# The shift of a modulation in PSUM columns of its own, without idle products, and a new hand-written job order in an attention and MLP kernel

## The chip, the cores and the metric

The kernel runs on one core of one Trainium2 chip. The metric is the time of one execution on the device, in microseconds. Five engines work beside each other, each through its own instructions in order: TensorE (PE, matrix products into PSUM), VectorE (DVE), ScalarE (ACT), GpSimd (POOL) and SyncE (SP), whose queue issues nearly all DMA transfers. PSUM has 8 banks of 512 fp32 columns.

## The reference

One transformer block with a modulation computed from a vector c. S = 2048 rows, D = 576 features, H = 32 heads of 18, Dff = 4608:

```
mod = silu(c) @ w_mod            # six vectors of 576: sa, ca, ga, sb, cb, gb
h = layernorm(x) * (1 + ca) + sa
q, k, v = split(h @ wqkv)        # per head, 18 wide
pq, pk = q @ w_phi, k @ w_phi    # per head, 18 x 18
phi_q = [softmax(pq), softmax(-pq)] ; phi_k likewise
kv = phi_k^T v ; z = sum over rows of phi_k
o = (phi_q kv) / (phi_q z + 1e-6) ; x = x + ga * (o @ wo)
h = layernorm(x) * (1 + cb) + sb
x = x + gb * (relu(h @ w1) @ w2)
```

## The kernel before, in words

The rows are 16 tiles of 128. The first part (up to about 90 us) is attention, the second (line 720 on) an MLP of eight blocks of two tiles, with two levels of a seven-product scheme. The change lies in the first part.

**Folded weights.** w_phi is folded into the Q and K weights on PE: `FK` (line 444, `fold_all`) makes the folded K weights in PSUM in 25 products, five for each of five chunks of features; `frd` and `fra` (line 455) copy chunk n to SBUF on DVE or ACT, `frr` (line 662) copies the rest of all chunks. `FQ n` (line 262) does the same for chunk n of Q, copied by `FQrd` or `FQra` (line 562).

**The norm without a normalized x.** x is loaded twice: in rows (`Lx..`, for the statistics `bn` on DVE, lines 243 and 244) and turned, features on partitions (`Lt0` to `Lt4`, for products). The turned x is multiplied by 1 + ca only, in place (`xd`, `xa`, `xp` on DVE, ACT or POOL, line 548, for two tiles at a time). Mean and standard deviation enter through four extra rows of the last of the five chunks of the contraction: on the x side they come from the statistics (`sa` on ACT, `sp` on POOL, `T` a transposition on PE, `Tc` a copy on ACT), on the weight side from products of the small matrix `m98` with the weights (`KR`, `VR`, `QR`, lines 273 and 369), whose rows are then put together by `KRh`, `KRd` and their like (lines 514 and 518). `m98` holds -(1 + ca) three times and the shift sa once (columns 96 to 99).

**The modulation.** `sx` (ACT) and `sd` (DVE, line 538) make silu(c). `sc` and `sh` (line 250, `mods`) are 25 products of one column each, for the scale ca and the shift sa, both into columns 0 to 4 of PSUM bank 7; ahead of each five of them stands an idle product of 512 columns (`spin`, line 236) into bank 6, which nothing reads. `ca` (line 543) reads the scale out of bank 7, adds 1, and writes -(1 + ca) to `m98`. `shc` (line 659) copies the shift to `m98`. `Z11` and `Z1` are idle products as well. The second modulation (`m2`, line 677) is made later.

**Tiles.** For each tile t: `K t` are ten products of 288 columns (line 279), `eK` two Exps on ACT (line 285), `sK` sums on DVE (line 291), `rK` reciprocals on ACT (line 307), `pA` and `pM` products on POOL, `V t` ten products, `vE` a product out of PSUM on DVE (line 312), `kv` nine products that accumulate over all tiles in banks 6 and 7, `Q t`, `eQ` like K. K of tile 0 and 1 is split: `Ka` (the first four chunks, eight products) and `Kb` (the last chunk, two products, which need the extra rows).

**What sets the order.** `ORDER` (line 45) is a list written out by hand; line 709 runs the jobs in that order, and each engine gets its instructions in it. `X:n` gives the job two PSUM banks, pair n. Semaphores are put in by the framework: an instruction waits for the writers of what it reads, and for the readers of what it overwrites. A load on SP also waits until the load eight places ahead of it on its ring has landed.

Of the kernel before, what the change touches and what calls it, by code (L numbers as in the profile page):

```python
# [18 lines left out]
NC = 5  # L19
R = 116  # L20
F = NC * R
FP = NC * F + P - R
X0 = 96
# [19 lines left out]


ORDER = """
Lbdw Z11 LwkT FK Z1 fra1 Lx0 Lcc sx bn0 sd frd2 Lwsc frd0 bn1 sa0 frr sc ca Lwsh frd4 Lx2 Lid bn3 sh fra3 sp0 T0:1 shc
Lt0 KR:2 KRh0 Lwv Lx4 xd0 bn2 KRh1 mk KRd0 KRd1 Tc0 sa2 Ka0:0 VR:1 bn4 VRh0 Kb0 VRd0 sp2 VRh1 Lt1 xd2 Ka1:2 Kb1 VRd1
T2:1 eKa0 sK0 LwqT FQ3:3 Tc2 K2:0 FQra3 bn5 Lwsb eKa1 sK1 K3:3 rK0 eK2 sa4 FQ4:2 FQrd4 pM0 V0:1 sK2 Lwcb rK1 pA1 pA0
Lt2 pM1 V1:0 m2:2 eK3 FQ0:3 Lx6 vE0 V2:1 Lwga vE1 rK2 Lx10 m2c FQrd0 pA2 FQ1:3 xa4 sp4 Lt4 bn7 vE2 T4:2 Tc4 K4:0 FQra1
eK4 FQ2:2 xp6 bn6 sa6 FQrd2 sK3 Lt3 bn11 K5:1 pM2 kv0 kv1 QR:2 eK5 V3:0 kv2 QRh sp6 QRe QRd T6:2 rK3 sK4 pA3 vE3 rp  # L50
Tc6 pM3 K7:1 rK4 K6:2 pM4 pA4 eK7 eK6 Lwgb ga:0 gac V4:1 bn9 kv3 sK5 rK5 bn8 pA5 w2b0 sa8 V5:2 vE4 bn12 sp8 T8:0 xa8
pM5 vE5 Tc8 Q0:1 eQ0 gb:2 xp14 kv4 kv5 sK6 bn10 Q1:0 gbc sa10 sK7 gaw gar wl1 rK6 K8:1 qs0 wl3 bn15 eQ1 eK8 K9:2 eK9
sp10 xp10 Lwo Q2:0 pA6 sK8 pM6 eQ2 V6:1 rK8 bn13 vE6 sK9 bn14 qp0 rK7 Q3:2 pA8 T10:0 Tc10 pA7 eQ3 qs1 pM7 kv6 K10:1
eK10 rK9 K11:0 sK10 pM8 V8:2 eK11 sa14 sa12 V7:1 vE8 pM9 rK10 V9:0 vE7 xa12 sp12 pA9 kv7 T12:2 sK11 rK11 kv8 V10:1 vE9
kv9 wl0 pA10 vE10 Tc12 pM10 K12:0 sp14 T14:2 Tc14 gbw eK12 kv10 K13:1 eK13 wo2 K14:2 eK14 qt0 qs2 sK12 sK13 Q4:0 eQ4
rK13 K15:1 w2a1 qp1 V11:2 V12:0 gbr qs3 wo1 pA11 qp2 pM11 vE11 kv11 w2a2 rK12 w2a0 pA12 eK15 vE12 sK15 pM12 qt1 V13:2
kv12 pM13 Lmask sK14 Q5:1 wl4 rK15 eQ5 sq5 Q6:0 pA13 pA15 vE13 sq4 kv13 qt2 V15:2 rK14 vE15 pM15 pA14 V14:1 vE14 eQ6
Q11:2 pM14 qp3 sq6 kv14 kv15 qt3 eQ11 sq11 Q7:1 kz nu1:2 Q8:0 nu0:3 nO1 td2 eQ7 eQ8 sq7 nO0 td0 sq8 ot1:2 td1 Q9:1 oc1
Q10:0 ot0:2 wo0 wo4 eQ9 qi5 wo3 sq9 oc0 eQ10 W1:3 xr1 qi4 W0:1 lb1 Q12:2 xr0 lb0 Q13:0 lr1 eQ12 sq10 qi6 lr0 ap1 eQ13
Q14:1 ht1:2 Q15:3 ap0 wl2 ht0:0 ha eQ14 eQ15 hd w2b1 sq13 sq15 sq14 sq12  # L60
"""

SEVEN = """
# [18 lines left out]
def tile_block(ctx, tc, a, out):  # L82
# [7 lines left out]
    def small(shape, dtype, name):  # L90
        return mem.tile(shape, dtype, name=name, tag=name)

    def carve(reg, start, shape):
        n = 1
        for d in shape:
            n *= d
        names = "abcd"[:len(shape)]
        v = reg[:, start:start + n]
        return v.rearrange(f"p ({' '.join(names)}) -> p {' '.join(names)}", **dict(zip(names, shape)))
# [21 lines left out]
    wsc, wsh, wkT, wqT = (R1[:, i * FP:(i + 1) * FP] for i in range(4))  # L121
# [8 lines left out]
    mk = small([P, 1], FP32, "mk")  # L130
# [4 lines left out]
    sc = carve(early, 1536, (4, P))  # L135
# [7 lines left out]
    m98 = carve(RS, NC * GR, (NC, NX))  # L143
# [28 lines left out]
    PS = psum.tile([P, 8, 512], FP32, name="PS")  # L172
# [6 lines left out]
    act, dve, pool, sp, pe = nc.scalar, nc.vector, nc.gpsimd, nc.sync, nc.tensor  # L179
# [56 lines left out]
    def spin(n, bank, w=512):  # L236
        for _ in range(n):
            pe.matmul(PS[:, bank, 0:w], lhsT=zero[:, 0:P], rhs=zero[:, 0:w], start=True, stop=True)  # L238
# [7 lines left out]
    def wide(w, ck, ci):  # L246
        o = ck * F + ci * R
        return w[:, o:o + P]

    def mods(w, bank, idle=None):  # L250

        o = PS[:, bank, :] if isinstance(bank, int) else bank[:, 0, :]
        for k, wm in enumerate(w):
            for ci in range(NC):
                if idle is not None:
                    spin(1, idle)
                for ck in range(NC):
                    wt = wide(wm, ck, ci) if len(wm.shape) == 2 else wm[:, ck, ci * P:(ci + 1) * P]
                    pe.matmul(o[:, k * NC + ci:k * NC + ci + 1], lhsT=wt[0:R],
                              rhs=siluc[0:R, ck:ck + 1], start=(ck == 0), stop=(ck == NC - 1))  # L260

    def fold_mm(wT, ck, pr):
# [181 lines left out]
    def fold_all(wT):  # L444

        for ck in range(NC):
            for g, (h0, nh) in enumerate(G7):
                nf, c0 = nh * DH, h0 * DH
                o = PS[:, ck, c0:c0 + nf] if g < 4 else PS[:, 5, FW * ck:FW * (ck + 1)]
                pe.matmul(o, lhsT=wide(wT, g, ck)[0:nf], rhs=bdw[0:nf, g, 0:nf], start=True, stop=True,  # L450
                          skip_group_check=True)
# [47 lines left out]
    T1, T2, T4 = (carve(RTh, i * TW, (NK, HD)) for i in range(3))  # L499
# [42 lines left out]

    def scale():
        dve.tensor_scalar(out=ca1[0:R, :], in0=PS[0:R, 7, 0:NC], scalar1=1.0, scalar2=None, op0=ALU.add)
        dve.tensor_scalar(out=m98[0:R, :, X0:X0 + 3], in0=ca1[0:R, :].unsqueeze(2).to_broadcast([R, NC, 3]), scalar1=-1.0,
                          scalar2=None, op0=ALU.mult)

# [94 lines left out]
    def k_minus(t):  # L642
# [10 lines left out]
    JOBS = {  # L653
        "Z": lambda i: spin(i, 6),
        "sx": lambda: act.activation(out=sg[0:R, 0, :], in_=ccol[0:R, :], func=ACT.Exp, scale=-1.0),
        "sd": silu, "ca": scale,
        "sc": lambda: mods([wsc], 7, idle=6),
        "sh": lambda: mods([wsh], 7, idle=6),
        "shc": lambda: dve.tensor_copy(m98[0:R, :, X0 + 3], PS[0:R, 7, 0:NC]),
        "FK": lambda: fold_all(wkT),  # L660
        "frd": lambda c: f_raw(dve, c), "fra": lambda c: f_raw(act, c),
        "frr": lambda: dve.tensor_copy(out=wk[0:R, :, G5:D], in_=last),
# [12 lines left out]
        "Q": lambda t: proj(at["Q", t], t, wq), "eQ": lambda t: exps(t, at["Q", t], EQ[:, SLOT[t], :]),  # L675
        "sq": q_out, "qi": q_in, "qs": q_sm, "qp": q_pool, "qt": q_turn,
        "m2": lambda: mods([wsb, wcb], at["m2", None]), "m2c": lambda: mod2_e(at["m2", None]),
        "wo": lambda c: pool.tensor_tensor(out=wo_sb[:, c, :], in0=wo_sb[:, c, :], in1=ga_row[:], op=ALU.mult),
        "wl": w1_part, "w2a": w2a_part, "w2b": w2b_part,
# [528 lines left out]
```

## Time and profile before

| | us |
|---|---|
| median of 3 runs | 375.18 (374.82 to 376.08) |
| the profiled execution | 374.84 |
| its span, first to last instruction | 373.1 |
| PE busy | 367.7 |
| DVE busy | 282.4 |
| ACT busy | 220.0 |
| first product of the MLP (line 732) starts at | 90.68 |

The page gives the busy time of each engine and 40 slices of the span; the chain of work that ended last tells, at each moment, whose work the end hung on; the timeline gives single instructions, with the idle time before them and what ended it in brackets. PE's matrix products are pipelined: two that follow each other start 0.12 us apart at 288 columns, though each is shown as 0.29 us long. The last slice of PE is not full because the output is added and written after the last product.

### The profile page before, as it was taken

To read this page: it belongs to the slowest core of one execution; us is meant where nothing else is said; L and a number is where in the kernel's file an instruction comes from. 1 tells how busy PE (TensorE), PEld (TensorE's weight loads), DVE (VectorE), ACT (ScalarE), POOL (GpSimd) and SP (SyncE) were. 2 spreads that over 40 slices of the span, in tenths; PEclk is the share of its full clock that TensorE was granted. 3 is DMA by queue.
4 is the path that set the end of the run, shared out by engine and by line. 5 is a ranking of instruction groups with operands and counts; after the bars stand their busy time and mean duration, and the time that the engine had idled before them with its cause. 6 is when DMAs were issued, how large, how long until landed. Compare 5 with 4: busy or idle time off the path is not lost.

```text
span 373.1 us, 14298 instructions
## 1 busy us (share of the span) xinstructions
PE 367.7 (99%) x6245; PEld 313.6 (84%) x6245; DVE 282.4 (76%) x508; ACT 220.0 (59%) x495; POOL 138.9 (37%) x203
## 2 busy tenths in 40 slices
PE   8999999999999999999999999999999999999996
PEld 4787888888888788889988987898799889979975
DVE  2999998679979779987795688578668747745752
ACT  2598998588633435608752774478167608844730
POOL 2167999840302567380054007102600240044023
DMA  8985799887966436463127236512521123101001
GB/s 296 414 362 154 271 411 315 218 238 296 265 187 132 125 81 152 126 133 95 36 46 182 35 35 83 147 37 52 128 52 20 37 50 37 35 0 36 4 2 33
DMA packets 58591, 49.96 MB, mean 134 GB/s; under 512 B 46880, under 2 KB 50848, under 8 KB 57760
## 3 DMA queue, kind: packets, MB, share of 16 engines
q1 hardware_dynamic: 58384, 48.88, 48.1%
q8 instruction: 49, 0.80, 0.9%
q10 hardware_dynamic: 144, 0.16, 0.1%
q14 instruction: 14, 0.11, 0.1%
HBM read 31.98 MB, written 5.90 MB: 102 GB/s over the span
## 4 chain that ended last, share of the span: by engine, by line
PE 96%; DVE 1%; ACT 1%; issue 0%; POOL 0%; DVEq 0%; POOLq 0%
PE PS L878 33%; PE PS L798 23%; PE PS L282 15%; PE PS L732 10%; PE PS L946 4%; PE PS L781 3%; PE PS L401 2%; PE PS L331 2%; PE PS L238 1%; PE PS L276 1%; PE PS L953 1%; PE PS L418 1%; PE PS L918 1%; ACT R L558 1%; DVE RH L459 0%; DVE st L243 0%
## 5 line engine op out<-in xcount | busy, mean ns | idle before, releaser
L878 PEld LDWEIGHTS <-RH 128*128 128x128 f16 x846 | 81.7, 98 | 21.2 <-issue 0.4
L866 POOL TENSOR_TENSOR yt<-yt,gb_row 128x288 f32<-128x288 f32 x23 | 27.5, 1194 | 176.1 <-DVE yt L865 176.1
L798 PEld LDWEIGHTS <-R 64*128 64x128 bf16 (+1 forms) x1824 | 76.0, 94 | 0.8 <-issue 0.2
L878 PE MATMUL PS<-R,RH 128*128 128x288 bf16 (+1 forms) x558 | 73.2, 286 | 0.0
L798 PE MATMUL PS<-h,R 64*128 64x128 bf16 x1056 | 69.2, 216 | 0.0
L828 ACT ACTIVATE RH<-PS 128x512 f16<-128x512 f32 x96 | 50.9, 605 | 9.2 <-PE PS L798 9.0
L798 PE MATMUL PS<-RE,R 64*128 64x128 f16 x768 | 48.1, 216 | 0.0
L287 ACT ACTIVATE RT<-PS,rs 128x576 bf16<-128x576 f32 x64 | 42.9, 744 | 3.6 <-PE PS L282 3.4
L878 PE MATMUL PS<-RT,RH 128*128 128x288 f16 x288 | 37.9, 286 | 0.0
L732 PE MATMUL PS<-h,R 64*128 64x256 bf16 (+1 forms) x684 | 36.3, 264 | 0.0
L732 PEld LDWEIGHTS <-R 64*128 64x128 bf16 x684 | 31.6, 94 | 3.9 <-issue 0.2
L975 ACT ACTIVATE h<-h,mod 128x256 bf16<-128x256 bf16 x63 | 32.5, 589 | 1.0 <-DMA h<-xn 1.0
L282 PE MATMUL PS<-RH,R 116*128 116x288 bf16 x240 | 32.7, 286 | 0.1
L798 PE MATMUL PS<-h,early 64*128 64x128 bf16 x384 | 32.0, 216 | 0.0
L282 PE MATMUL PS<-RH,RT 116*128 116x288 bf16 x240 | 31.5, 286 | 0.0
L818 ACT ACTIVATE yt<-PS 128x512 f32<-128x512 f32 x10 | 6.0, 597 | 42.7 <-PE PS L798 41.8
L243 DVE BATCH_NORM_STATS2 st<-x_sb 128x6 f32<-128x288 bf16 x64 | 25.7, 443 | 6.3 <-DMA x_sb<-in_xk_dram 6.2
L865 DVE TENSOR_TENSOR yt<-PS,RS 128x288 f32<-128x288 f32 x23 | 10.5, 456 | 23.4 <-PE PS L878 23.3
L282 PEld LDWEIGHTS <-R 116*128 116x128 bf16 x240 | 22.6, 98 | 6.2 <-ACT R L626 0.4
L282 PEld LDWEIGHTS <-RT 116*128 116x128 bf16 x240 | 22.9, 98 | 5.5
L798 PEld LDWEIGHTS <-w 64*128 64x128 f16 (+1 forms) x480 | 26.4, 94 | 0.0
L867 POOL TENSOR_TENSOR x_sb<-yt,x_sb 128x288 bf16<-128x288 f32 x30 | 24.9, 833 | 3.5 <-DVE yt L863 1.7
(153 smaller groups left out, 737.9 us busy)
## 6 DMA issues: line engine op xcount, KB each, us to landing
R<-in_w_dram SPq DMA_DIRECT2D x4, 1152.0 KB
eqd<-RT SPq DMA_DIRECT2D x12, 288.0 KB, 3.6
RT<-eqd SPq DMA_DIRECT2D x12, 288.0 KB, 3.1
R<-in_w2b_dram SPq DMA_DIRECT2D x2, 1296.0 KB, 6.7
R<-in_w2a_dram SPq DMA_DIRECT2D x3, 864.0 KB
out_dram<-x_sb SPq DMA_DIRECT2D x15, 144.0 KB, 1.8
RT<-in_xT_dram SPq DMA_DIRECT2D x2, 640.0 KB, 6.5
x_sb<-in_xk_dram SPq DMA_DIRECT2D x8, 144.0 KB, 3.6
```

The costliest lines, as they stand in the source:

```text
L243: dve.bn_stats(out=s[:, hf, :], in_=x_sb[:, t % 8 if n else t, hf * HD:(hf + 1) * HD])
L282: pe.matmul(pr[:, k, 0:HD], lhsT=xt(t, ck), rhs=w[0:R, ck, k * HD:(k + 1) * HD], start=(ck == 0), stop=(ck == NC - 1))
L287: act.activation(out=E.rearrange("p (b h s e) -> p b h s e", b=2, s=2, e=DH)[:, :, :, s, :], in_=pr[:, :, 0:HD].rearrange("p b (h e) -> p ...
L732: pe.matmul(PS[:, 2 * u + hf, n * 256 + o:n * 256 + o + w], lhsT=w1_lhs(hf, c, j, h), rhs=hb[b0:b0 + 64, c, o:o + w], start=(n == 0 and c ...
L781: pe.matmul(PS[:, bank_at[n], j * 256:j * 256 + 256], lhsT=w1_lhs(hi, c, j, hi), rhs=hb[64 * hi:64 * hi + 64, c, :], start=(j == 0 and c = ...
L798: pe.matmul(PS[:, bank_at[BK[n] + str(g)], i * P:(i + 1) * P], lhsT=w[r, (4 * c + i) * P:(4 * c + i + 1) * P], rhs=x, start=(n in ("M1", " ...
L828: act.activation(out=o, in_=v[{"k11": "Y", "k12": "Z", "k21": "X", "k22": "W"}[n]], func=ACT.Relu)
L866: pool.tensor_tensor(out=y, in0=y, in1=gb_row[:, c], op=ALU.mult)
L867: eng.tensor_tensor(out=xs(t)[:, c], in0=y, in1=xs(t)[:, c], op=ALU.add)
L878: pe.matmul(PS[:, bank, 0:HD], lhsT=am[:, j, :], rhs=bm[:, j, :], start=first and j == 0, stop=(j % 9 == 8), skip_group_check=True)
L946: pe.matmul(pr[:, k, 0:HD], lhsT=oT[:, t % 2, ci, :], rhs=wo_sb[:, ci, k * HD:(k + 1) * HD], start=(ci == 0), stop=False, skip_group_check ...
L975: act.activation(out=o, in_=o, func=ACT.Identity, scale=mod(1, c), bias=mod(0, c))
```

## The change

It does four things. The idle products of `sh` go. `sh` writes columns 8 to 12 of bank 7 instead of 0 to 4, and `shc` reads them there. The job `ca` is split: `ca` makes 1 + ca, a new job `cm` writes the negated copies to `m98`. And ORDER is a new list, in which among much else the turned x of tiles 0 and 1 (`Lt0`) is loaded ahead of the shift's weights (`Lwsh`), `sx` stands ahead of the fold, the turned x of tiles 4 to 7 (`Lt2`) is loaded ahead of the second modulation's weights, and the first four chunks of K of tile 0 (`Ka0`) come before the m98 products of K (`KR`).

```diff
 ORDER = """
-Lbdw Z11 LwkT FK Z1 fra1 Lx0 Lcc sx bn0 sd frd2 Lwsc frd0 bn1 sa0 frr sc ca Lwsh frd4 Lx2 Lid bn3 sh fra3 sp0 T0:1 shc
-Lt0 KR:2 KRh0 Lwv Lx4 xd0 bn2 KRh1 mk KRd0 KRd1 Tc0 sa2 Ka0:0 VR:1 bn4 VRh0 Kb0 VRd0 sp2 VRh1 Lt1 xd2 Ka1:2 Kb1 VRd1
-T2:1 eKa0 sK0 LwqT FQ3:3 Tc2 K2:0 FQra3 bn5 Lwsb eKa1 sK1 K3:3 rK0 eK2 sa4 FQ4:2 FQrd4 pM0 V0:1 sK2 Lwcb rK1 pA1 pA0
-Lt2 pM1 V1:0 m2:2 eK3 FQ0:3 Lx6 vE0 V2:1 Lwga vE1 rK2 Lx10 m2c FQrd0 pA2 FQ1:3 xa4 sp4 Lt4 bn7 vE2 T4:2 Tc4 K4:0 FQra1
-eK4 FQ2:2 xp6 bn6 sa6 FQrd2 sK3 Lt3 bn11 K5:1 pM2 kv0 kv1 QR:2 eK5 V3:0 kv2 QRh sp6 QRe QRd T6:2 rK3 sK4 pA3 vE3 rp
-Tc6 pM3 K7:1 rK4 K6:2 pM4 pA4 eK7 eK6 Lwgb ga:0 gac V4:1 bn9 kv3 sK5 rK5 bn8 pA5 w2b0 sa8 V5:2 vE4 bn12 sp8 T8:0 xa8
-pM5 vE5 Tc8 Q0:1 eQ0 gb:2 xp14 kv4 kv5 sK6 bn10 Q1:0 gbc sa10 sK7 gaw gar wl1 rK6 K8:1 qs0 wl3 bn15 eQ1 eK8 K9:2 eK9
+Lbdw LwkT Lx0 Lcc sx Z11 Lwsc Lt0 Lwsh Lx2 Lid FK Lwv frd0 fra3 bn1 sd frd4 frr Lt1 mk bn0 sa0 Lx4 sp0 Z1 sc frd2 LwqT
+ca xd0 sh shc fra1 Ka0:2 cm KR:3 KRh0 Lt2 bn3 KRh1 bn2 Lwsb KRd0 T0:0 KRd1 Tc0 VR:1 xd2 sa2 Lwcb Lx6 VRh0 VRd0 bn4 Kb0
+Ka1:0 VRh1 Kb1 eKa0 VRd1 sp2 T2:1 Tc2 K2:3 FQ0:1 sK0 K3:2 eKa1 eK2 FQ1:0 V1:3 rK0 sK1 FQrd0 FQ4:1 bn5 FQra1 FQrd4 rK1
+pA1 Lt3 pM1 V0:0 eK3 sa4 sp4 pA0 vE1 xa4 sK2 m2:1 FQ2:3 vE0 V2:2 FQrd2 bn6 m2c pM0 rK2 pA2 vE2 bn7 FQ3:0 T4:1 Tc4
+FQra3 K4:3 eK4 QR:1 sa6 Lt4 pM2 QRh sK3 QRe K5:0 kv0 eK5 sK4 xp6 V3:2 Lx10 sK5 rK3 sp6 Lwgb kv1 kv2 QRd rK4 T6:0 Tc6
+pA3 K7:1 vE3 bn9 rK5 bn8 xp10 eK7 K6:0 eK6 bn13 pA5 Lwga V5:2 pM3 pA4 vE5 sa8 sp8 V4:1 vE4 w2b0 Q0:0 T8:1 Q1:2 xa8 Tc8
+rp ga:1 pM4 kv3 eQ0 sK6 K8:0 xp14 sK7 eQ1 bn11 rK6 gac pM6 K9:2 kv4 eK8 gb:1 eK9 gbc w2a2 Q2:0 qs1 pM5 V6:1 bn10 pA6
...
 """
-    def mods(w, bank, idle=None):
+    def mods(w, bank, idle=None, at0=0):
...
-                    pe.matmul(o[:, k * NC + ci:k * NC + ci + 1], lhsT=wt[0:R],
+                    pe.matmul(o[:, at0 + k * NC + ci:at0 + k * NC + ci + 1], lhsT=wt[0:R],
...
     def scale():
         dve.tensor_scalar(out=ca1[0:R, :], in0=PS[0:R, 7, 0:NC], scalar1=1.0, scalar2=None, op0=ALU.add)
+
+    def minus_scale():
         dve.tensor_scalar(out=m98[0:R, :, X0:X0 + 3], in0=ca1[0:R, :].unsqueeze(2).to_broadcast([R, NC, 3]), scalar1=-1.0,
                           scalar2=None, op0=ALU.mult)
...
-        "sd": silu, "ca": scale,
+        "sd": silu, "ca": scale, "cm": minus_scale,
         "sc": lambda: mods([wsc], 7, idle=6),
-        "sh": lambda: mods([wsh], 7, idle=6),
-        "shc": lambda: dve.tensor_copy(m98[0:R, :, X0 + 3], PS[0:R, 7, 0:NC]),
+        "sh": lambda: mods([wsh], 7, at0=8),
+        "shc": lambda: dve.tensor_copy(m98[0:R, :, X0 + 3], PS[0:R, 7, 8:8 + NC]),
```

The rest of ORDER, up to the first MLP product, is new too, with the same jobs; its last three lines are, before and after:

```
Q11:2 pM14 qp3 sq6 kv14 kv15 qt3 eQ11 sq11 Q7:1 kz nu1:2 Q8:0 nu0:3 nO1 td2 eQ7 eQ8 sq7 nO0 td0 sq8 ot1:2 td1 Q9:1 oc1
Q10:0 ot0:2 wo0 wo4 eQ9 qi5 wo3 sq9 oc0 eQ10 W1:3 xr1 qi4 W0:1 lb1 Q12:2 xr0 lb0 Q13:0 lr1 eQ12 sq10 qi6 lr0 ap1 eQ13
Q14:1 ht1:2 Q15:3 ap0 wl2 ht0:0 ha eQ14 eQ15 hd w2b1 sq13 sq15 sq14 sq12
...
kv13 pM15 sq7 vE14 kv14 kv15 kz wo2 sq4 Q6:2 eQ6 nu0:0 qp3 nO0 qt3 wo0 wo4 Q8:1 nu1:3 ot0:2 gbr sq6 qi4 eQ8 oc0 qi5
nO1 Q9:0 ot1:3 oc1 Q10:1 eQ10 eQ9 W1:2 td1 sq10 td2 qi6 sq9 td0 xr1 lb1 W0:3 Q12:2 sq8 lr1 eQ12 xr0 lb0 lr0 wl4 sq12
Q13:0 eQ13 Q14:3 ap1 ht1:2 Q15:1 ap0 ht0:0 hd ha eQ15 sq13 eQ14 w2b1 sq15 sq14
```

Here `kz` masks the accumulated kv (line 612), `nu` and `nO` are numerator and quotient of tiles 0 and 1, `W` their output products, `Q4` to `Q15` keep Q of the later tiles, and `wl`, `w2a`, `w2b` load the MLP's weights.

More of the change, by code (lines that the diff above doesn't have):

```diff
@@ L51 @@
-Tc6 pM3 K7:1 rK4 K6:2 pM4 pA4 eK7 eK6 Lwgb ga:0 gac V4:1 bn9 kv3 sK5 rK5 bn8 pA5 w2b0 sa8 V5:2 vE4 bn12 sp8 T8:0 xa8
-pM5 vE5 Tc8 Q0:1 eQ0 gb:2 xp14 kv4 kv5 sK6 bn10 Q1:0 gbc sa10 sK7 gaw gar wl1 rK6 K8:1 qs0 wl3 bn15 eQ1 eK8 K9:2 eK9
-sp10 xp10 Lwo Q2:0 pA6 sK8 pM6 eQ2 V6:1 rK8 bn13 vE6 sK9 bn14 qp0 rK7 Q3:2 pA8 T10:0 Tc10 pA7 eQ3 qs1 pM7 kv6 K10:1
-eK10 rK9 K11:0 sK10 pM8 V8:2 eK11 sa14 sa12 V7:1 vE8 pM9 rK10 V9:0 vE7 xa12 sp12 pA9 kv7 T12:2 sK11 rK11 kv8 V10:1 vE9
-kv9 wl0 pA10 vE10 Tc12 pM10 K12:0 sp14 T14:2 Tc14 gbw eK12 kv10 K13:1 eK13 wo2 K14:2 eK14 qt0 qs2 sK12 sK13 Q4:0 eQ4
@@ L56 @@
[L56 to L60, printed above, removed]
+Lbdw LwkT Lx0 Lcc sx Z11 Lwsc Lt0 Lwsh Lx2 Lid FK Lwv frd0 fra3 bn1 sd frd4 frr Lt1 mk bn0 sa0 Lx4 sp0 Z1 sc frd2 LwqT
@@ new lines @@
+rp ga:1 pM4 kv3 eQ0 sK6 K8:0 xp14 sK7 eQ1 bn11 rK6 gac pM6 K9:2 kv4 eK8 gb:1 eK9 gbc w2a2 Q2:0 qs1 pM5 V6:1 bn10 pA6
+wl2 sa10 bn12 rK7 eQ2 Q3:2 wl0 sp10 sK9 T10:0 rK9 Tc10 vE6 kv5 Lwo pM7 gaw gar Lmask K10:1 qs0 kv6 pA9 bn15 eQ3 K11:0
+qp1 pM9 V7:2 bn14 pA7 eK10 sa12 sa14 wl1 V10:1 sK8 sK10 eK11 rK10 sp12 vE7 qp0 pA10 V8:0 rK8 pA8 V9:2 kv7 vE10 sp14
+vE8 T12:1 xa12 Tc12 qt1 K12:0 vE9 pM8 kv8 T14:2 K13:1 pM10 eK12 wo1 sK11 rK11 Tc14 kv9 eK13 wl3 K14:0 Q4:2 eK14 V11:1
+pM11 eQ4 qs2 qp2 qs3 sK12 sK13 rK12 pA11 rK13 pM13 gbw kv10 K15:0 eK15 pA12 vE11 wo3 kv11 sK14 Q5:1 rK14 pM14 V12:2
@@ L61 @@
+w2a0 sK15 rK15 vE12 eQ5 pA14 Q7:0 pA15 qt0 pA13 V13:2 eQ7 vE13 w2a1 V15:1 V14:0 pM12 vE15 qt2 sq5 Q11:1 eQ11 sq11 kv12
+kv13 pM15 sq7 vE14 kv14 kv15 kz wo2 sq4 Q6:2 eQ6 nu0:0 qp3 nO0 qt3 wo0 wo4 Q8:1 nu1:3 ot0:2 gbr sq6 qi4 eQ8 oc0 qi5
+nO1 Q9:0 ot1:3 oc1 Q10:1 eQ10 eQ9 W1:2 td1 sq10 td2 qi6 sq9 td0 xr1 lb1 W0:3 Q12:2 sq8 lr1 eQ12 xr0 lb0 lr0 wl4 sq12
+Q13:0 eQ13 Q14:3 ap1 ht1:2 Q15:1 ap0 ht0:0 hd ha eQ15 sq13 eQ14 w2b1 sq15 sq14
 """
```

## The prediction

> **What bounds the kernel now.** I read the page first, then the chain of work that ended last for the first 95 us, then the timeline of the first 30 us, and last the busy time by stage. The page says that TensorE (PE) is the engine that is never free, and that only its first and last slices are not full:
>
> ```profile
> PE 367.7 (99%) x6245; PEld 313.6 (84%) x6245; DVE 282.4 (76%) x508; ACT 220.0 (59%) x495; POOL 138.9 (37%) x203
> ...
> PE   8999999999999999999999999999999999999996
> ```
>
> A busy PE may still be padding or waiting inside, so I asked the chain where PE is not the one that is followed. Its columns are the start, the length (us) and the piece of work. The opening is the one long place:
>
> ```profile
> 8.31 1.18 DVE RH L459 x2
> 9.49 0.74 DVE st L243 x2
> ...
> 10.25 0.21 DVE mv L244
> 10.46 0.40 DVE RH L662
> 10.86 0.08 DVE ca L544
> ...
> 11.03 0.18 DVE RS L545
> 11.21 0.58 DVE RH L459
> 11.79 0.74 DVE st L243 x2
> ...
> 12.55 0.21 DVE mv L244
> 12.76 0.09 DVE RS L659
> ...
> 12.89 1.43 PE PS L276 x10
> ```
>
> See that from 8.31 to 12.85 the chain is VectorE (DVE) alone, and that the products of m98 with the K weights (L276) wait for DVE's copy of the shift (L659). All that PE does in this time is filling. The timeline shows the shift's own products, the idle products between them, and what they waited for:
>
> ```profile
> 9.86 0.38 PE L238 MATMUL PS<-early 128*128 128x512 bf16 x1
> ...
> 10.98 0.26 PE L259 MATMUL PS<-siluc,R 116*128 116x1 bf16 x5 [0.74 <-DVE ca L544]
> ...
> 11.11 0.38 PE L238 MATMUL PS<-early 128*128 128x512 bf16 x1
> ```
>
> The stages show the rest (PE, PEld, DVE, ACT, POOL busy):
>
> ```profile
> 12.89:28.40 15.51, 15.36 (x177) 12.62 (x177) 15.15 (x35) 13.35 (x38) 6.80 (x16) 1.00 0.92 375
> 28.40:90.68 62.28, 62.28 (x696) 50.89 (x698) 53.89 (x89) 52.44 (x123) 46.20 (x87) 1.00 0.82 267
> ```
>
> From 28.40 on PE is full to the end of the attention part (the first L732 product starts at 90.68), and the chain after it is PE almost without a break. So a new order there can only lose. It can win in two places: the start of unbroken work (12.89), and the gaps behind it. From the starts of products in PE's timeline, against an unbroken spacing of 0.123 us for 288 columns, these gaps are 0.08 and 0.11 (near 18.0 and 18.4), 0.07 (19.5), 0.20 (22.4), 0.10 (26.5) and 0.28 (28.0): 0.84 us.
>
> **The change, part by part.** Five idle products of 512 columns go (0.22 us each, two start at 7.64 and 7.86): 1.1 us of PE, all of it between 11.11 and 12.35, while PE waits for DVE anyway. On the path they are worth nothing; the cover is DVE's line of L545, L459, L243, L244 above, which ends 0.1 us after them.
>
> *Columns of its own.* They should let the shift's products run beside DVE's read of the scale. In the built order of the changed kernel the first of them still waits for that read (the `ca` instruction), as before. I take this edit at 0; if the wait were gone, the shift would be ready 1 us earlier and DVE would still reach its copy no sooner, so 0 is the other end as well.
>
> *DVE's line up to the products.* I lay the new order out with the spacings of DVE's rows: L459 0.59, an L243 pair with its L244 0.98, the three of `sd` 0.51, L662 0.40, L560 0.196 each, L659 0.08, L545 0.13. The Exp of `sx` now precedes the fold, so `sd` need not wait for it (0.4 us in before). `frd0` can start when the first fold group is done (the fourth L450 product ends at 6.59): 6.62. bn1 7.21, sd 8.18, siluc ready for PE at 8.82 (before: 8.37, so the scale's products are 0.45 later and end at 10.46), frd4 8.69, frr 9.28, bn0 9.67, frd2 10.64, `ca` 11.23 (before 10.78). The shift's 25 products then start at 11.43 and, at 0.025 us each, PE is free at 12.06. DVE goes on with five x scalings from 11.48, the shift's copy at 12.46 and the -scale at 12.54, done by 12.75. DVE's line is as long as before: bn3 leaves it, five scalings enter.
>
> *What PE does instead.* It no longer needs the shift to start: Ka0, eight products of tile 0, needs only the scaled x (first chunk at 11.8, fourth at 12.4) and K weights 0 to 3 (ACT's last one ends near 11.9). So unbroken work begins at 12.06, and lasts 0.98 us, to 13.04, where the -scale has long been there. That is 0.83 earlier than 12.89, less the two transposes T0 (0.11) that before had done by then: 0.72.
>
> *Loads.* Turned x of tiles 0 and 1 (320 KB) goes ahead of the shift's weights (728 KB). At 414 GB/s (second slice) it takes 0.8 us, so the shift's weights, whose first weight load is seen at 9.90, come by 10.7, ahead of 11.43. The Q weights stay behind the same bytes and their issue still follows the landing of the scale's weights (8.12). x of tiles 4 to 7 (640 KB, 1.6 us) now goes ahead of the second modulation's weights: their products move from 25.1 at the end to about the same time, and the loads end near 23.5 (the last landed at 21.9 in before, plus 1.6), wanted at 24.4. No cost, slack 0.9 us. The issues held behind the second modulation's two small copies on SP are x of tiles 12 to 15 and later ones, wanted after 36; the moved row copies of Q (L536) land before their chunk at 38.
>
> *Gaps in the new order.* I laid out each engine's jobs by hand to the end of K5, with ACT's pair of Exps at 1.25, L292 1.26, L313 0.66, L521 0.55, POOL's L299 1.12 and its small ones from their rows. PE waits for: KRd1 0.04; T2 for VRd0 0.17; V1 for eK2, whose bank pair it takes, 0.34 (ACT does eKa0, Tc2, eKa1, eK2 in a row from 16.5 to 20.8); FQ4 for FQrd0 0.08; m2 for FQrd4 0.11; K4 for FQrd2 0.06. Sum 0.80, against 0.84 in before. So at 30 us the lead is 0.72 + 0.04, some 0.8.
>
> *From 30 to 90 us.* The same layout, coarser, has ACT dense up to 48 and PE waiting 0.1 us for eQ0 before K8 and less at K9; comparing with the chain, where T10 starts at 48.94 with one 0.35 us kv more done, mine starts at 48.16: a lead of 0.43. The difference of the two (0.4) is what such a sum is worth. Behind it ACT and DVE fall idle by themselves in before, and the order of the last ten jobs (kz, the numerators, W, L1) leaves the same work between writer and reader. I take 0.6, the middle of 0.43 and 0.8. Bounds: all gaps gone, 0.72 + 0.84 = 1.6; none of the lead kept and every new wait lost, below.
>
> After 90.68 nothing of the code changes and PE is dense. The last large load is now the half as big one (576 KB against 1152 KB), which no wait of before asks for: 0.
>
> **Sum.** The profiled execution took 374.84 us (span 373.1 and 1.7 around it), 0.34 under the median of 375.18. Its sum is 374.84 - 0.6 = 374.2; against the median, which I predict, 374.6.
>
> **Rivals.**
> *ACT hands over late (slower).* Between 15 and 48 us ACT has no pause in the new order, and xa8 (five L558, 2.0 us) stands right ahead of Tc8 and eQ0, eQ1, while Q0 and Q1 now come before K8, gb and V6. Slack on PE at FQ4, m2, K4, T8, K8 and K9 is under 0.1 us each. It decides once ACT or DVE is 0.1 late; if each of the six is then 0.3 late (a wait of the size of V1's), that is 1.8: 374.6 + 1.8 = 376.4. For it: ACT 4.89 of 5 us at 20 to 25. Against it: before runs as dense and loses 0.84.
> *The clock falls without the idle products (slower).* The opening's 11 products of 512 columns took 4.88 us, 0.43 apart; the two at 7.64 are 0.22 apart, and the fold's spacing falls from 0.106 to 0.058 near 6.7, so PE starts at half speed and needs 5.4 us of work to leave it. In before the longest stretch without a large product is 9.86 to 11.11. Now it is from about 10.3 to 12.06 with 25 one-column products in it. If half speed came back there, dense work would run at half for up to 5.4 us: 2.7 lost, 377.3. Against it: the granted clock is 1.00 in every stage, and 0.7 us idle at 10.2 did no harm. [...] Whether one-column products count as work, no run here shows.
> *The gaps close (faster).* If the layout is pessimistic and PE waits for nothing after 12.06: 374.6 - 1.0 = 373.6.
> *The change does nothing where it says.* The shift keeps its wait, ACT sets the pace, the lead is used up by 48 us: 375.2.
>
> **Chances.** A measurement of this kernel can tell about 0.3% (1.1 us) from no change. Forecast 374.6 (374.0 to 375.0): 0.47. Lead used up, 375.2: 0.18. ACT late, 376.4: 0.15. Clock, 377.3: 0.06. Gaps close, 373.6: 0.14. Only the last is faster by over 0.3% (374.05), with a part left within: faster 0.13; the two slow ones 0.21; the same 0.66. The range goes from 373.5 to 376.5 and leaves out the clock and the ends.
>
> **What would show it.** First L282 product at 12.1 and L276 at 13.0; the shift's first product waiting for `ca` until 11.4; a wait of some 0.3 before V1, less elsewhere; first L732 product at about 90.1. An L282 spacing of 0.24 instead of 0.12 after 12 us would mean the clock; waits of PE for L287 or L564 in 35 to 50 us would mean ACT. The forecast is wrong if PE has over 1 us of waits between 30 and 90 us, which my coarse layout cannot exclude.

## The result and the profile after

The changed kernel took 378.68 us (median of 4 runs, 377.52 to 382.9), beside 375.0 for the kernel before on the same chip: a ratio of 1.0113, 95% interval 1.0077 to 1.0149. It is slower, by 1.1%; the prediction had said 374.6 with a range up to 376.5. The profiled execution took 378.84 (span 377.0), 4.0 more than that of before (374.84).

Below, L734, L744, L759, L948, L600 and L604 are lines 732, 742, 757, 946, 598 and 602 of the kernel before, and two marks on the way divide the loss: the first product of the MLP (L734) and the first product of the projection in its first block (L948).

| profiled execution, us | MLP starts | projection starts | first to second | whole |
|---|---|---|---|---|
| before | 90.6 (read as 90.68 in the prediction) | 105.6 | 15.0 | 374.84 |
| changed | 91.7 | 109.1 | 17.4 | 378.84 |

So 1.1 us are lost ahead of the MLP and 2.4 more in the first level of its first block. From the projection to the last product both need 264.3. The last 0.5 lie behind the last product, where the issue of a store of the output took 1.49 us instead of 0.45; one execution shows this, and I did not follow it up.

**The opening.** The page of the changed kernel has a line that the page of before does not have, the granted clock of PE in 40 slices (PEclk):

```profile
PE   7999999999989999999999999999999999999996
...
PEclk9899999999999999999999999999999999999999
```

One slice, the second, is at 8, all others are at 9. The trace of before holds no record of the clock, so there it has to be read from the spacing of products: its L276 products (12.89 to 14.16) start 0.12 us apart, which is the unbroken spacing. The changed kernel's PE timeline in this slice (start, length, work, and in brackets idle time and what ended it):

```profile
10.97 0.78 PE L259 MATMUL PS<-siluc,R 116*128 116x1 bf16 x25 [0.86 <-DMA R<-in_wsh_dram]
11.61 1.65 PE L282 MATMUL PS<-RH,R 116*128 116x288 bf16 x8
13.05 2.59 PE L276 MATMUL PS<-RH,RS 116*100 116x288 bf16 x10
```

The ten L276 products, which took 1.43 in before, take 2.59. The stages, cut at the clock's own records in the trace, say why (busy times, then third from the end the granted clock):

```profile
8.67:12.09 3.42, 2.48 (x55) 1.89 (x53) 3.35 (x15) 1.07 (x4) 0.16 (x2) 1.00 1.02 410
12.09:15.50 3.41, 3.41 (x17) 2.67 (x15) 2.32 (x8) 0.40 (x1) 0.97 (x6) 0.50 1.02 414
15.50:18.91 3.41, 3.41 (x31) 2.95 (x30) 2.73 (x10) 3.12 (x9) 0.24 (x1) 1.00 1.02 418
```

For exactly one stretch of 3.41 us the clock was half. 14 products in it are 0.24 us apart instead of 0.12: 14 x 0.118 = 1.65 us. What DVE's line of before (8.31 to 12.85) has become: its copy of the shift is done at 12.03 and its -(1 + ca) at 12.10, well ahead of the L276 products. DVE no longer holds the opening. The two stages of the prediction, from the first L276 product on, cut at the changed kernel's own marks:

```profile
13.05:28.40 15.35, 14.89 (x171) 12.36 (x169) 13.45 (x28) 12.75 (x37) 4.99 (x14) 0.92 0.77 315
28.40:91.68 63.28, 63.03 (x694) 51.20 (x692) 54.60 (x92) 53.32 (x123) 48.11 (x88) 1.00 0.87 271
```

The clock of the first is 0.92, and PE is now free for 0.46 and 0.25 us where it was for 0.15 and 0.

**Level 1.** PE's timeline of the changed kernel, further on:

```profile
98.53 6.73 PE L734 MATMUL PS<-h,R 64*128 64x256 bf16 x120 [0.42 <-issue]
106.98 2.19 PE L734 MATMUL PS<-h,R 64*128 64x256 bf16 x36 [1.73 <-DVE RH L744]
109.10 2.13 PE L948 MATMUL PS<-wo_sb,oT 128*128 128x288 bf16 x16
```

In before PE has no break between 90.6 and the projection; the same products stand there in one dense row:

```profile
95.55 10.16 PE L732 MATMUL PS<-h,R 64*128 64x256 bf16 x180
```

In the changed kernel PE waits for a relu on DVE (L744), and DVE had waited ahead of that. DVE's timeline, and then SP's waits from 82 to 106 us (line, what it waited for, sum, times, longest):

```profile
103.77 0.56 DVE L759 TENSOR_TENSOR RT<-RH 128x768 f16<-128x768 f16 x1 [2.90 <-ACT RH L742]
```

```profile
SPq L346 <- DMA eqd<-RT: 4.0, 2, 3.5
```

L759 is the first sum of level 1. It writes over memory (RT) in which the Exps of Q stood, so it also waits until their stores to `eqd` have landed. The view names ACT, which was done long before; the last of these stores landed at 103.64, and the sum started at 103.77. The traces of e1 and e11 below name the store itself in this place. Why the stores were late is seen in SP's queue. In the changed kernel:

```profile
84.83 0.32 SPq L343 DMA_DIRECT2D eqd<-RT  x1
88.76 0.32 SPq L346 DMA_DIRECT2D RT<-eqd  x1
89.13 0.91 SPq L343 DMA_DIRECT2D eqd<-RT  x2
90.08 0.48 SPq L604 DMA_DIRECT2D R<-in_w_dram  x1
91.00 1.01 SPq L343 DMA_DIRECT2D eqd<-RT  x2
92.11 0.40 SPq L600 DMA_DIRECT2D R<-in_w2b_dram  x1
94.54 1.58 SPq L343 DMA_DIRECT2D eqd<-RT  x2
```

and in before:

```profile
84.35 0.32 SPq L343 DMA_DIRECT2D eqd<-RT  x1
86.87 0.32 SPq L346 DMA_DIRECT2D RT<-eqd  x1
87.26 0.41 SPq L602 DMA_DIRECT2D R<-in_w_dram  x1
87.78 0.37 SPq L598 DMA_DIRECT2D R<-in_w2b_dram  x1
89.11 6.92 SPq L343 DMA_DIRECT2D eqd<-RT  x4
```

The L346 line is `qi6`, the fetch of tile 6's Q. It goes into the memory out of which `sq10` (the store ahead of it) reads, so it waits until that has landed: from 85.2 to 88.7 SP stands, and all behind it stands. In before SP stands at this fetch too, but for 2.1 us, and the two stores of tiles 8 and 9 had gone out ahead of it. The loads of w1 (L604) and w2 (L600) went out 2.8 and 4.3 us earlier there. The DMA engines show the consequence; what they moved in GB/s, in 40 slices of 84 to 106 us (0.55 each), changed kernel:

```profile
GB/s 352 323 356 344 243 63 42 21 0 0 84 142 339 405 402 327 115 92 243 327 369 415 470 419 427 425 471 358 369 432 360 238 162 72 60 169 170 8 215 0
```

and before:

```profile
GB/s 222 293 335 287 13 0 21 121 348 465 385 436 452 400 425 415 452 320 426 283 300 409 394 415 400 352 205 107 226 224 6 8 120 276 285 131 184 83 136 31
```

In the changed kernel the engines run dry in slices 6 to 12, until 90.6; against some 400 GB/s, as in slices 14 and 15, that is an estimated 1.3 MB not moved. Before has a dry stretch too (slices 5 to 8, 0.8 MB), but it is over at 88.4. The w2 load of 1296 KB goes out at 92.1 and then stands ahead of the last two stores: issued at 94.5 and 95.8, they land at 102.25 and 103.64. In before the last ones, issued at 94.7 and 95.6, landed at 98.36 and 99.75.

### The profile page after: what moved, and what is told of

Read it like the earlier page. It is cut to its first block, busy times and chain, and to the rows that moved or that the text cites. A ratio compares the mean times of both kernels' runs of the same rounds, so it can differ in the third digit from the quotient of the medians.

```text
span 377.0 us, 14280 instructions
## 1 busy us (share of the span) xinstructions
PE 367.7 (98%) x6239; PEld 314.6 (83%) x6240; DVE 282.1 (75%) x508; ACT 220.4 (58%) x495; POOL 139.0 (37%) x203
## 4 chain that ended last, share of the span: by engine, by line
PE 71%; DVE 0%; issue 0%
PE PS L880 32%; PE PS L800 23%; PE PS L734 6%; PE PS L948 4%; PE PS L783 3%; PE PS L401 1%; PE PS L955 1%; PE PS L920 1%; DVE x_sb L921 0%; DVE R L512 0%
## 5 line engine op out<-in xcount | busy, mean ns | idle before, releaser
L734 PE MATMUL PS<-h,R 64*128 64x256 bf16 (+1 forms) x684 | 36.5, 264 | 2.1 <-DVE RH L744 1.7
L734 PEld LDWEIGHTS <-R 64*128 64x128 bf16 x684 | 32.5, 94 | 5.5 <-issue 2.5
L884 ACT ACTIVATE RS<-PS 128x288 f32<-128x288 f32 x24 | 9.9, 411 | 27.7 <-PE PS L880 27.7
```

Of the source, the lines that this page charges most:

```text
L734: pe.matmul(PS[:, 2 * u + hf, n * 256 + o:n * 256 + o + w], lhsT=w1_lhs(hf, c, j, h), rhs=hb[b0:b0 + 64, c, o:o + w], start=(n == 0 and c ...
```

## The experiments

Two theories came out of the traces. **Clock**: without the idle products the opening holds too little work and the clock falls, 1.65 us. **Queue**: the fetch `qi6` stands 3.5 us in SP's queue, loads and stores come late, and the first sum of level 1 waits, 2.3 us. Rivals: that these are one loss seen twice; that the late w2 load alone makes the second; that the columns of their own or the new order of the work do it. Medians and ratios are each against the kernel before on the same chip (375.0 to 375.3).

| | MLP starts | projection | median | ratio (95%) |
|---|---|---|---|---|
| changed | 91.7 | 109.1 | 378.68 | 1.0113 (1.0077 to 1.0149) |
| e1_idle4 | 90.2 | 109.4 | 379.12 | 1.0097 (1.0068 to 1.0125) |
| e2_w2b | 91.6 | 110.0 | 380.71 | 1.0160 (1.0132 to 1.0188) |
| e3_both | 90.3 | 110.0 | 378.80 | 1.0095 (1.0071 to 1.0120) |
| e4_code | 92.1 | 107.7 | 376.77 | 1.0046 (1.0029 to 1.0064) |
| e5_tail_idle4 | 97.8 | 112.6 | 382.10 | 1.0175 (1.0155 to 1.0195) |
| e6_tail | 98.7 | 113.6 | 382.10 | 1.0189 (1.0170 to 1.0208) |
| e7_columns_idle | 90.1 | 105.7 | 375.29 | 1.0009 (0.9990 to 1.0027) |
| e8_before_late_w2b | 90.5 | 105.5 | 375.22 | 1.0000 (0.9991 to 1.0010) |
| e9_queue_idle4 | 90.4 | 105.5 | 375.24 | 1.0004 (0.9989 to 1.0019) |
| e10_queue | 91.6 | 107.8 | 376.56 | 1.0036 (1.0020 to 1.0051) |
| e11_before_w2b_at_end | 90.7 | 109.6 | 379.30 | 1.0117 (1.0090 to 1.0144) |
| e12_queue_idle4_v1 | 91.5 | 106.4 | 376.34 | 1.0034 (1.0019 to 1.0048) |

**e1, e2, e3: one loss each, then both.** e1 is the changed kernel with four idle products ahead of the shift's; e2 moves the w2 load ahead of `sq10`; e3 does both.

```diff
-ca xd0 sh shc fra1
+ca xd0 Z4 sh shc fra1
```
```diff
-W1:2 td1 sq10 td2 qi6
+W1:2 td1 w2b1 sq10 td2 qi6
```

> The changed kernel (378.7 us) with four idle products of 512 columns put between the scale's and the shift's products, where TensorE waits for the shift's weights anyway (9.9 to 10.9 us). Theory A (removing the idle products lets the clock fall for one window of 3.4 us): no half-clock stretch is left, the products of m98 stand 0.12 us apart again instead of 0.24, and the time falls by about 1.65 to 377.0. Rival B (the clock's fall is a chance of this execution, or the dense work after it only waits later): the fall stays, or goes and the time stays at 378.7.

> The changed kernel with the last load of the MLP's second weights (1296 KB) moved on SP's queue from behind the store of tile 13's Q to ahead of that of tile 10's. Theory A (issued at 92.1 us, it delays the two last Q stores to 102.3 and 103.6, for which the first sum U2 of the MLP waits, and DVE's and then TensorE's stop of 1.9 us follows): U2's sum starts by 101, the stop of 1.9 us goes, and the time falls by 1.5 to 2.4, to 376.3 to 377.2. Rival B (the transfers are simply too many there, wherever the load stands): the stores land as late, time 378.5.

> Both edits at once. Theory A: the two losses add up, 1.65 + 2, and the time is 374.6 to 375.3, level with the kernel before or a little faster; the clock does not fall. Rival (a third loss, ScalarE handing over late in the new order, carries the difference): 376.5 or more.

In e1 the opening keeps its clock, the dense products are 0.12 apart, and the MLP starts at 90.2, 1.5 earlier than in the changed kernel and 0.45 earlier than in before. But the projection still starts at 109.4. The earlier PE waits longer in level 1, and then the clock falls there. DVE's first sum, for which the view here names the store, PE's timeline, and the stages, cut at the clock's records:

```profile
102.75 0.56 DVE L759 TENSOR_TENSOR RT<-RH 128x768 f16<-128x768 f16 x1 [3.11 <-DMA eqd<-RT]
```

```profile
105.97 3.54 PE L734 MATMUL PS<-h,R 64*128 64x256 bf16 x36 [2.59 <-DVE RH L744]
```

```profile
103.10:106.52 3.42, 0.83 (x17) 0.62 (x13) 3.42 (x6) 0.87 (x2) 0.00 (x0) 1.00 1.36 125
106.52:109.93 3.41, 3.41 (x33) 2.54 (x28) 2.23 (x5) 0.42 (x2) 0.00 (x0) 0.50 1.06 281
```

So the 1.5 us are lost again in two parts. The last store lands 1.0 us earlier than in the changed kernel (102.63 instead of 103.64), so PE goes on only 1.0 us earlier (105.97 instead of 106.98): 0.5 went into the wait. The fall then takes the rest and more, since the 36 products after the stop need 3.54 us instead of 2.19. It does not come each time. Of e1's four executions the one with a granted clock of 1.00 throughout took 377.28, close to the 377.0 expected (its trace is not kept); the other three (0.994 and 0.995) took 378.85 to 379.42.

e2 went against my theory as I first had it, that the late w2 load makes the loss. The load goes out early, but `sq10` now lands behind its 1296 KB, at 92.5, so that `qi6` and all behind it stand 7.4 us; PE stops for 2.3, 1.0 and 0.4 us from 95.5 on, the first two for Exps of Q on ACT, which wait 3.3 us for stores to `eqd`. e3 is missed as well: 378.80, where 374.6 to 375.3 was expected. Its queue stands for 7.2 us and PE stops as in e2, and the clock falls from 98.01 to 101.42. Its rival, ScalarE handing over late, came true in the figure only, since ACT itself waits 3.4 us for those stores. So it is the order of the queue around the fetch that has to change, and not the place of one load.

**e4 and e7: the code alone, in the order of before.** Both take the order of before, with the columns of their own and `cm` right behind `ca`; e4 drops the shift's idle products, e7 keeps them (the first of the two new lines of `sh` is e4's, the second e7's).

```diff
-frr sc ca Lwsh
+frr sc ca cm Lwsh
...
-        "sh": lambda: mods([wsh], 7, idle=6),
+        "sh": lambda: mods([wsh], 7, at0=8),      
+        "sh": lambda: mods([wsh], 7, idle=6, at0=8),
```

> The code change alone on the order of before: shift in columns 8 to 12 without idle products, the negated copy in a job of its own right behind the scale. Theory A: the longest stretch without a large product is now 10.2 to 12.9 us, the clock falls for a window, and the time is 1.0 to 2.0 over before: 376 to 377. Rival (a low stretch of TensorE here does not matter, the new order does it): 375.0, as before.

> The order of before, the shift in columns 8 to 12 and the negated copy in a job of its own, but the five idle products kept. Against the run without them (376.8, half clock for 3.4 us) this is the idle products alone. Theory A: clock never halved, 375.0, columns of their own bring nothing. Rival (the fall has to do with the other edits): 376.7.

Without the idle products the clock falls in this order too, from 13.73 to 17.15 (stages of e4):

```profile
13.73:17.15 3.42, 3.42 (x17) 2.53 (x15) 3.10 (x9) 1.67 (x6) 0.61 (x3) 0.50 1.05 424
```

With them it stays at 1.00 and the time is that of before. All four executions of e4 have a granted clock of 0.994 or 0.995. The idle products are thus worth 376.77 - 375.29 = 1.5 us, and the columns of their own nothing that can be measured. e7 shows one thing more. Its MLP starts 0.5 us earlier than in before, yet the projection starts no earlier; PE waits for it (timeline):

```profile
105.74 2.13 PE L948 MATMUL PS<-wo_sb,oT 128*128 128x288 bf16 x16 [0.52 <-DMA oT<-o_sb]
```

The projection needs the turned outputs (oT), the end of a chain of stores, fetches and transposes on SP of its own. In before PE starts the projection at 105.64 without a wait; when the chain is ready there, no view shows. In e7 a lead at the MLP's start is worth nothing, because that chain is not early too.

**e5, e6: the fetch ahead.** The changed kernel with `qi6` right behind `qi5` and the w2 load ahead of `sq12`; e5 has four idle products as well. In both, tile 10's Exps write over what the fetch of tile 6's Q brought, so that what these two compute for tile 6 is not the reference.

```diff
-qi4 eQ8 oc0 qi5 nO1
+qi4 eQ8 oc0 qi5 qi6 nO1
...
-W1:2 td1 sq10 td2 qi6 sq9
+W1:2 td1 sq10 td2 sq9
...
-lr0 wl4 sq12
+lr0 wl4 w2b1 sq12
```

> The changed kernel with the four idle products, and on SP's queue the fetch of tile 6's Q moved ahead of the store of tile 10's (in the changed kernel it waited 3.5 us for that store to land, and everything behind it waited too) and the last 1296 KB load put ahead of the stores of tiles 12 to 15. Theory A' (the clock, and SP standing still behind that fetch so that loads and stores are issued late): the MLP starts at 90.2, no stop of over 0.5 us in the first level of its first block, the clock stays, 374.3 to 375.0. Rival B' (the tail's transfers are bound by bandwidth, not by their issue): the stop stays near 106, time 377 or more.

> The same queue order without the four idle products. Theory A': only the clock's fall in the opening is left, 1.5 over the run with idle products: 376.0 (375.7 to 376.5). Rival B': 378.5, as the changed kernel.

Both lose more, elsewhere: the Exps of tile 10 now wait for the fetch, whose place in memory they need (5.75 us in e6), and hold a pair of banks. PE's timeline of e6 (the wait is 4.59 in e5):

```profile
91.12 4.96 PE L282 MATMUL PS<-RH,RT 116*128 116x288 bf16 x20 [4.28 <-ACT RT L287]
```

During this stop the clock falls in both, and it stays at half for 6.83 us. Neither of their theories' times came. From the MLP's start to the projection both need 14.9 us: the stop in level 1 is gone, though their MLP also starts 6 to 7 us later, which gives the stores more time, so that this alone does not decide. The fetch is tied to tile 10 from both sides, so it has to stay where it is, and the others have to go ahead of it.

**e9, e10: the others ahead of the fetch.** The changed kernel with another order of SP's jobs alone; e9 also has the four idle products.

```diff
-qi5 nO1 Q9:0 ot1:3 oc1 Q10:1 eQ10 eQ9 W1:2 td1 sq10 td2 qi6 sq9 td0
+qi5 sq8 nO1 Q9:0 ot1:3 oc1 Q10:1 eQ10 sq10 eQ9 sq9 wl4 w2b1 qi6 W1:2 td1 td2 td0
...
-Q12:2 sq8 lr1 eQ12 xr0 lb0 lr0 wl4 sq12
+Q12:2 lr1 eQ12 xr0 lb0 lr0 sq12
...
-sq13 eQ14 w2b1 sq15 sq14
+sq13 eQ14 sq15 sq14
```

> The changed kernel with four idle products ahead of the shift's, and with SP's queue in another order: the store of tile 8's Q behind the fetch of tile 5's, those of 10 and 9 right behind their Exps, then the last w1 load, the w2 load and only then the fetch of tile 6's Q, which waits for the store of tile 10's to land. Theory (the queue stood 3.5 us behind that fetch, the DMA engines ran dry meanwhile, and loads and stores that came late landed late): no stop of PE in level 1 of the MLP, from its start to the projection 15.0 us as in the kernel before (the changed kernel: 17.4), MLP from 90.2, time 374.5, ratio 0.9987. Rival (the stop comes from the MLP's earlier start, which needs the sums and stores sooner, whatever the queue): a stop of over 1 us at 100 to 105, 377 or more.

> The same order of SP's queue without the four idle products. If the fall of the clock in the opening costs its 1.65 us by itself: MLP from 91.7, 15.0 us to the projection, 376.1, ratio 1.003. If the two losses are one (the late opening is made up while the MLP waits for its stores anyway): as e9_queue_idle4, within 0.5 us.

PE's timeline of e9:

```profile
95.30 10.25 PE L734 MATMUL PS<-h,R 64*128 64x256 bf16 x180
105.48 2.13 PE L948 MATMUL PS<-wo_sb,oT 128*128 128x288 bf16 x16
```

The stop is gone (0.2 us remain at 96.4), the last stores land at 98.6, and from the MLP to the projection it is 15.1 us. SP still stands at the fetch, for 2.4 us (86.97 to 89.33), but the two loads and the stores of tiles 8, 9 and 10 are now ahead of it. The rival, that an earlier MLP must wait anyway, falls. The time is 375.24, that of before, and not the 374.5 of my theory: the lead at the MLP is 0.25, at the projection 0.16, at the last product 0.06.

e10, without the idle products, is 1.3 us above e9 and 2.1 below the changed kernel. So with the queue mended the clock costs 1.3 us, and the queue costs 2.1 beside the fallen clock; together 3.4 of the 3.7 between the medians. They are two losses, and not one seen twice. The changed kernel's four executions spread over 5.4 us, so the 2.1 is rough; e1's execution with the clock kept, 377.28, lies 2.0 above e9. By the medians e1 lies 3.9 above e9, the second fall of the clock included. In ten of e10's twelve executions the granted clock is 0.995, and the one with 1.00 is the fastest, 375.63. e10's profiled execution (377.32, its slowest) also had a stop of 1.2 us at 97.7 of which the profile names no releaser, so that from the MLP to the projection it is 16.2 and not the expected 15.0; in the changed kernel this stop was 0.4. What that is stays open.

**e8, e11: a late load in the kernel before.** e8 moves the w2 load one store later (behind `sq13`), e11 two (behind `sq15`).

```diff
-hd w2b1 sq13 sq15 sq14 sq12
+hd sq13 w2b1 sq15 sq14 sq12
```
```diff
-hd w2b1 sq13 sq15 sq14 sq12
+hd sq13 sq15 w2b1 sq14 sq12
```

> The kernel before with one edit: the last 1296 KB load goes from ahead of the store of tile 13's Q to right behind it, its place in the changed kernel. Theory A' (the last Q stores land later and the first U2 sum waits for them): the sum starts 1 to 2 us later than 99.87 and the time grows by 0.3 to 1.5. Rival (the place of that load is indifferent as long as SP does not stand still ahead of it): 375.0.

> The kernel before with one load moved: w2's 1296 KB behind the store of tile 15's Q, so that the last two stores of Q stand behind it, as they stand behind the late loads in the changed kernel. Theory (late loads ahead of the last stores make these land late, and the first sum of level 1 over their memory waits): the stores land at about 103.5 instead of 99.75, a stop of PE of 1.5 to 2 us at about 104, time 376.5 to 377, ratio 1.004 to 1.005. Rival (it is the standing fetch alone, and late loads cost nothing): 375.0 to 375.3.

e8 changes nothing in the time: its load still goes out some 5 us ahead of the last stores. The last of these lands 0.9 us later (100.62), and PE has no stop. In e11 the load goes out at 95.24. Behind it stand `sq14`, issued at 95.68, and `sq12`, issued at 96.17, and the sum starts at 104.26, when the store it waits for has landed. This must be `sq14`, since `sq12` lands later, at 104.85. DVE's group (busy, mean, idle ahead and what ended it) and PE's timeline:

```profile
L757 DVE TENSOR_TENSOR RT<-RH 128x768 f16<-128x768 f16 x1 | 0.6, 558 | 4.4 <-DMA eqd<-RT 4.4
```

```profile
107.47 2.14 PE L732 MATMUL PS<-h,R 64*128 64x256 bf16 x36 [2.92 <-DVE RH L742]
```

Here the view names the store itself. This shows, in the order of before, with the clock at 1.00 in the profiled execution and with the fetch waiting hardly longer than in before (2.4 us), the second half of the chain: a large load close ahead of the last stores makes them late, and the first sum waits. It costs 4.2 us, more than I expected: the sum starts 0.8 us later than the landing at 103.5 that I had taken, the stop of 2.9 is 0.9 longer than the longest expected, and PE also stops for 0.6 at 93.7 for a load of w1, a wait that I did not foresee and have not followed.

**e12: the wait ahead of V.** e9 with V of tile 1 one job later.

```diff
-FQ1:0 V1:3 rK0 sK1 FQrd0 FQ4:1 bn5
+FQ1:0 rK0 sK1 FQrd0 FQ4:1 V1:3 bn5
```

> As e9_queue_idle4, with the products of V for tile 1 one job later, behind the fourth round of the fold, so that their bank's Exps of K are read out by then. If the wait of 0.53 us ahead of V goes: MLP from 89.7, 374.0, ratio 0.9973. If the fold's round waits for the copy of its bank instead, as long: 374.5, as e9_queue_idle4.

Neither theory's figure came. The wait of 0.5 ahead of V is gone, and the fold's fourth round, which takes its place, waits 1.6 for the copy of its bank on DVE (timeline):

```profile
22.31 0.43 PE L267 MATMUL PS<-RS,R 126*128 126x126 bf16 x6 [1.64 <-DVE RH L568]
```

V had covered that copy. The MLP starts 1.1 us later than in e9, and the time is 1.1 more. I found no version that beats the kernel before.

## Why the prediction was wrong

The size and the sign failed at two steps; most of the layout of the opening held.

- **"After 90.68 nothing of the code changes and PE is dense ... 0."** This failed, and costs 2.1 us by e10 against the changed kernel (2.0 with the clock kept). The code after 90.68 is the same, but what it waits for is issued ahead of it. I had followed the last large load by its size and asked whether a wait of before names it; I had not written down SP's queue, in which `sq8` and `sq9` fell behind `qi6`, the w1 load behind these, and the w2 load behind two more stores. The prediction itself says that behind 28.40 a new order "can only lose", and still puts this loss at 0. Nor did the sentence "leaves the same work between writer and reader" (for the last ten jobs) hold: it looked at PE, ACT and DVE, not at SP.
- **Five idle products: "On the path they are worth nothing".** This failed too, and costs 1.3 us (e10 against e9) to 1.5 (e4 against e7). Their time was indeed covered (four of the five start between 11.11 and 12.14, the first at 9.86), but they had a second use, the clock. The rival for this had a chance of 0.06 and should have had far more. Its argument against itself, that 1.00 is granted in every stage of before, was no evidence: that trace holds no record of the clock, and the view gives 1.00 from 0 to 5 us too, where the idle products start 0.43 us apart. Its price, 2.7 for up to 5.4 us at half clock, was too high: the trace has 1.65 over 3.41 us. PE was not idle for long ahead of the fall: from 8.67 to 12.09 it was busy for 2.48 of 3.42 us. But 48 of its 55 products there are one column wide, and whether such products count as work the prediction left open; counted at their columns, this stretch holds 1.27 us (last section).
- **Unbroken work from 12.06.** Right in kind, and better in time: the first K product starts at 11.61, since `ca` came at 10.64, not 11.23. The L276 products start at 13.05 at half clock; with the clock kept they start at 12.66 (e1) and 12.82 (e9), where I had 13.04.
- **What the shift's products wait for.** I said `ca`, until 11.4. They waited for their own weights, until 10.97: the load came 0.3 later than my 10.7. It cost nothing.
- **Columns of its own: 0.** Right: e7 against before, 1.0009 (0.9990 to 1.0027).
- **Gaps, 0.80.** They came to about 0.9 up to K5 and 0.4 ahead of K8: V of tile 1 waits 0.62 for eK2, not 0.34, and K8 waits 0.42 for eQ0, not 0.1. The rival of ACT handing over late thus exists, at about a quarter of its price. The sign by which the forecast was to be known as wrong, over 1 us of waits between 30 and 90, did not come; the loss lay ahead of that stretch and behind it.
- **A lead of 0.6 at 90 us.** With the clock kept it is 0.45 (e1) and 0.25 (e9). That it is then worth 0.6 us of time was wrong: in e7 it is gone by the projection, which waits for a chain of its own, and in e9 0.16 of the 0.25 are left there and 0.06 at the last product. The case "lead used up, 375.2" has the figure that the change gives when both losses are mended (375.24), but by luck, since the lead shrinks behind the MLP's start and not by 48 us.

So the forecast of 374.6 comes to the measured 378.7 in three steps: 0.6 for the lead that is no time (e9, 375.2), 1.3 for the clock (e10, 376.6) and 2.1 for the queue.

## What to carry to other kernels

When a list of jobs is reordered, write down the new queue of SP as well, with the wait of each transfer: here one that waited for a landing held all behind it for 3.5 us, and its price fell due some 18 us later (from 85.2 to 103.8), where memory is used again. Idle products are taken out only after a look at how much work is left in each stretch of 3.41 us (the length of a fall here), one-column products counted at their columns: in these traces half clock followed stretches with at most 1.27 us. And before time is won ahead of a stage, look up what else that stage waits for, since a lead over another chain is spent waiting (0.5 us in e7). A granted clock of 1.00 in a trace without records of the clock says nothing (before: 1.00 from 0 to 5 us, with 512 columns 0.43 apart instead of 0.22); the spacing of equal products does.

## What the runs showed of the hardware

**In these traces half clock followed windows with few columns streamed.** Thirteen traces have records of the clock (the changed kernel and the experiments). Ahead of the last product, falls last 3.413 us (seven) or 6.827 us (two, in e5 and e6), and they lie on a grid of 3.413 us that starts at another place in each execution (the fall of the opening begins at 12.09 in the changed kernel and at 13.73 in e4). I added up, for each window of this grid at full clock, the columns of its products at 0.42 ns each (512 columns are 0.22 us apart), and counted once what two products of 64 rows stream side by side (36 of 256 columns take 2.19 us, 0.06 each). In five traces one idle product near 9 us has a weight load but no record of its own; it is counted. The falls behind the last product, all after windows with at most 1.08 us of columns, are left out.

| us of columns in the window of 3.41 | next window |
|---|---|
| 0, 0.35, 0.40, 0.86, 1.06, 1.12, 1.25, 1.26, 1.27 | half clock, 9 of 9 |
| 1.53, 1.64, 1.73, 1.78, 1.79 and all fuller ones | full clock |

The window of the changed kernel (8.67 to 12.09) is the one with 1.27. The profile calls PE busy there for 2.48 of 3.42 us, but 48 of its 55 products are one column wide. In e12 the window from 20.85 to 24.26 is busy for only 1.95 us, with 1.91 us of columns, and the clock stays. So in these traces the limit lies between 1.27 and 1.53 us of columns, a share of 37% to 45%, and PE's busy share does not tell it. The place on the grid made a difference as well. In the profiled executions e11's stop of 2.9 us lies across two windows, with PE busy for 1.90 and 2.01 us, and brings no fall, while e1's of 2.6 lies inside one, with PE busy for 0.83, and brings a fall; in four of e11's six executions the granted clock is 0.994 or 0.995. With the idle products a fall is rare but not excluded: one of e7's ten executions and three of before's 55 in the experiments have a granted clock of 0.991 to 0.995.
